# Attention and FFN on one core: the next pair's score products move behind the first FFN piece of the step

## The chip, the core and the metric

The kernel runs on one core of a Trainium2 chip. It uses the five engines of the core (TensorE for matrix products, VectorE, ScalarE, GpSimd, and SyncE, which here only issues transfers) and the 16 DMA engines. The metric is the device time of one execution in microseconds, lower being better. The kernel before takes 714.4 us, the median of three runs.

## The reference

Attention over 4 batches, 8 heads, 576 positions and 64 channels, with a bias that a small network of the distance of two positions makes for every head, and behind it a feed-forward network (FFN) on the 2304 tokens of 512 channels, with a hidden size of 2048:

```python
scores = scale * np.matmul(q, k.transpose(0, 1, 3, 2))
x = (np.log1p(np.abs(rel)) / psi_i)[..., None]
bias = np.maximum(x @ w1 + b1, 0.0) @ w2
scores = scores + bias.transpose(2, 0, 1)[None, :, :, :]
scores = scores - np.max(scores, axis=-1, keepdims=True)
attn = np.exp(scores)
attn = attn / (np.sum(attn, axis=-1, keepdims=True) + 1e-09)
x = np.matmul(attn, v)            # heads side by side: 2304 x 512
h = x @ w_in
g = h * np.clip(h + 3.0, 0.0, 6.0) / 6.0
out = g @ w_out
```

## The kernel before

**Tiles.** The 8 heads of a batch are taken two at a time (`PAIRS`). A unit is one batch, one pair of heads and either the first 256 query positions (4 tiles of 128 rows) or the last 320 (5 tiles). The 16 units of four tiles come first, then the 16 of five, 144 tiles in all. Tiles 2k and 2k+1 of a unit are the two heads of the same 128 positions, and their score products are made together, as a **pair** of tiles; the fifth tile of a long unit holds the last 64 positions of both heads and is a **single**. The order in a long unit is thus first pair, second pair, single.

**A step.** The main loop runs once for each tile number n. `front(n)` takes the row maximum of tile n on VectorE (`soft_max`, L561, which reads the scores out of PSUM together with the bias), emits the score products of the next pair if tile n+1 begins one (`qk_step(n + 1)`, L549 for tiles in two parts of fp32r, L527 for the first units), then normalizes tile n-1, makes the low half of tile n-2, sends tile n-3 through a transposing transfer (`soft_turn`, L637, issued by SyncE), and, where tile n-5 was the last of its unit, multiplies the unit's probabilities with v (`pv_step`, L704, **PV** below). `x_high` and `x_low` (L718 on ScalarE, L138 on VectorE) read PV's result a step later as two fp16 halves of x. Behind `front` the loop emits a part of the bias network where there is some left (`bias_step`, L864), and then pieces of the FFN: `rf` or `rf1` of them in a step (2.0, or 1.55 in the long units, carried over as `credit`). A piece is 12 matmuls: for the first half, one block of h (`h_ps`, L779), for the second, four blocks of the sum over the hidden size of an output block (`o_ps`, L802). `back(n)` does `x_high` and the exponential of tile n (L572).

**What sets the order.** Up to step 45 (`SWITCH`) a planner with a timeline of its own orders all engines. From then on, the steady part, TensorE runs in the order in which the program emits the work (`keep_order("PE")`), and from step 45 (`spn`) SyncE's queue does too. VectorE, ScalarE and GpSimd are still ordered by the planner. Each engine runs its list from top to bottom, and an instruction that waits holds up what is behind it.

**Banks.** In the steady part PSUM is split by `open_psum(ctx, 2, 4)`: two score tiles of two banks each, and four banks that h_ps, o_ps, PV and the bias take in turn. A pair takes both score tiles, a single one; they go round in turn. `reuse_waits="tile"` lets a tile be written again when all that read it is done: for a score tile that is L561, for PV's bank `x_low`, for h_ps L762 on VectorE.

Of the kernel before, what the change touches and what calls it, by code (L numbers as in the profile page):

```python
# [33 lines left out]
def attention_moe_kernel(  # L34
# [45 lines left out]
    def s_bank(name):  # L80
        return pools["ps_s"].tile([128, 2, 512], F32, tag="s", name=name)

    out_open = [False, 0]
    steady = [False]
    queue = []
# [423 lines left out]
    def at(n):  # L509
        return 0 <= n < NT  # L510
# [7 lines left out]
    def qk_step(n):  # L518
        b, p, t = tiles[n]
        i, s = ORDER[t]  # L520
        u = int(t >= 4)
        if direct(b, p, t):
            ps = s_bank("s_ps")
            q, k = qk_t[b, p, 0]
            c = 256 * s + 128 * i
            for a in range(2):
                nc.tensor.matmul(  # L527
                    out=ps[:, a, 0:HALF], lhsT=q[:, c:c + 128], rhs=k[:, a * HALF:(a + 1) * HALF]
                )
            s_t[n] = ps  # L530
            return
        if s:
            return
        if i == 4:
            hi, lo, tz = qk_t.pop((b, p, u))
            every = slice(0, 128)
            parts = [(every, tz[:, 0], tz[:, 1])]
        else:
            hi, lo = qk_t[b, p, u][:2]
            c = QC0[u] + 128 * i - 256 * u  # L540
            qs = slice(c, c + 128)
            parts = [(r, hi[r, qs], lo[r, qs]) for r in (slice(0, 64), slice(64, 128))]
        for k in range(len(parts)):
            s_t[n + k] = s_bank("s_ps")
        for k, (q, m) in enumerate(((0, hi), (0, lo), (1, hi))):
            for a in range(2):
                cs = slice(KC0[u] + a * HALF, KC0[u] + (a + 1) * HALF)
                for j, (rows, *w) in enumerate(parts):
                    nc.tensor.matmul(  # L549
                        out=s_t[n + j][:, a, 0:HALF], lhsT=w[q], rhs=m[rows, cs],  # L550
                        start=(k == 0), stop=(k == 2),
                    )

    def soft_max(n):
        b, p, t = tiles[n]
        i, s = ORDER[t]
        out, src = bt_t[b, p, i]
        bt, src = out[:, s * S:(s + 1) * S], src[s]
        ps = s_t.pop(n)[:, :, 0:HALF]
        sm = sm_p.tile([128, 4], F32, tag="sm", name="sm")  # L560
        nc.vector.tensor_tensor_reduce(  # L561
            out=halves(bt), in0=ps, in1=halves(src), op0=ALU.add, op1=ALU.min,
            scale=-0.125, scalar=3.0e38, accum_out=sm[:, 0:1],
        )
        a_t[n] = (bt, sm)
# [34 lines left out]
    def direct(b, p, t):  # L600
        return b < cfg["fb"] and t < 4
# [329 lines left out]
    def front(n):  # L931
        late = at(n + 1) and not direct(*tiles[n + 1])
        if at(n + 1) and not late:
            qk_step(n + 1)
        if at(n):
            soft_max(n)
        if n == START:
            open_ffn()
        if n == SWITCH:
            open_steady()  # L940
        if late:
            qk_step(n + 1)
        if unit_at(n - 6):
            x_low(*unit_at(n - 6))
        if at(n - 1):
            soft_norm(n - 1)
        if at(n - 2):
            soft_low(n - 2)
            if tiles[n - 2][2] in (1, 3, 5, 7, 8):
                freed[0] += 1  # L950
        if at(n):
            aux(n)
        if at(n - 3):
            soft_turn(n - 3)
        if unit_at(n - 5):
            pv_step(*unit_at(n - 5))
        while len(bt_t) - freed[0] < 4 and len(bt_t) < len(keys):
            k, b, p, i = keys[len(bt_t)]
            if k - n > cfg["la"]:
                break  # L960
            bias_until(256 if i < 2 else S)
            bt_t[b, p, i] = load_bias(b, p, i)
        if unit_at(n - 6) and unit_at(n - 6)[1] == PAIRS - 1:
            return unit_at(n - 6)[::2]
        return None

    def back(n):
        if unit_at(n - 5):
            x_high(*unit_at(n - 5))
        if at(n):  # L970
            soft_exp(n)
# [125 lines left out]
    def open_ffn():  # L1097
        nonlocal phase
        drain(gen_w)
        hidden_scale(0)  # L1100
        for c in range(KC):
            xv = x_t[0, 0][:, :, c]
            nc.vector.tensor_scalar(
                out=xv, in0=xv, scalar1=pscale["r1"][:, c:c + 1], scalar2=None, op0=ALU.mult
            )
        if cfg["fb"] > 1:
            x1 = const.tile([128, KC], F32, name="x1")
            nc.vector.tensor_scalar(
                out=x1, in0=pscale["r1"], scalar1=pscale["v1"][1], scalar2=None, op0=ALU.mult
            )  # L1110
            pscale["x1"] = x1
        stack_a.close()
        del pools["a"], pools["w"]
        pools["g"] = ctx.enter_context(tc.tile_pool(name="g", bufs=1, reuse_waits="tile"))
        pools["f"] = ctx.enter_context(tc.tile_pool(name="f", bufs=2, reuse_waits="tile"))
        queue.append(ffn(0, 0))
        phase = 1

    def open_steady():
        nonlocal phase  # L1120
        while phase < 2:
            ffn_step()
        stack_p.close()
        open_psum(ctx, 2, 4)
        steady[0] = True
        keep_order("PE")
# [27 lines left out]
    for n in range(-1, NT + 7):  # L1154
        if n < 7:
            next(gen_v, None)
        if n == cfg["spn"]:
            keep_order("SP")
        done = front(n)
        if phase == 0:  # L1160
            steps(gen_w, aw, cfg["rw1"])
        else:
            ao[0] += cfg["ro"]
            while ao[0] >= 1.0:
                ao[0] -= 1.0
                out_ready = not out_step()
        if phase and out_steps[0] >= cfg["bo"]:
            steps(gen_b, ab, cfg["rb"])
        if done is not None and done != (0, 0):
            b, u = done  # L1170
            queue.append(ffn(b, u))
        if queue:
            if phase == 1.5 and not out_ready:
                credit = cfg["gap"]
            else:
                credit += cfg["rf0"] if phase == 1 else cfg["rfo"] if phase < 2 else cfg["rf1" if unit_no[min(n, NT - 1)] >= 16 else "rf"]
            while credit >= 1.0 and queue and (phase < 2 or steady[0]):
                if ffn_step():
                    credit -= 1.0
                if phase == 1.5 and not out_ready:  # L1180
                    break
        back(n)
    for q_ in queue:
        drain(q_)
# [57 lines left out]
```

## Time and profile before

| | |
|---|---|
| median of three runs | 714.4 us (710.62 to 718.45) |
| the profiled execution's own time | 713.93 us |
| its span, first to last instruction | 712.1 us |
| TensorE matmuls busy | 657.8 us, 92% |
| VectorE, ScalarE, GpSimd busy | 498.2, 491.8, 257.0 us |
| h_ps matmuls (L779), o_ps matmuls (L802) | 198.6 and 196.6 us |
| mean granted TensorE clock | 0.976 |

The busy share is a mean over stages. The first 240 us make the bias, convert the weights and start the attention; the steady part follows up to about 600 us; then the rest of the FFN runs alone. In the rows below a time is counted from the start of the span, and an engine's idle time stands in brackets with what ended it.

### The profile page before, as it was taken

The numbers are of one execution on the slowest core, as the hardware profiler recorded it, in microseconds if no ns is written. First come the engines' busy times: TensorE is split into PE (matmuls) and PEld (weight loads), VectorE is DVE, ScalarE is ACT, GpSimd is POOL, SyncE is SP. The second block draws the span as 40 slices with busy tenths as digits, with TensorE's granted clock in tenths as the row PEclk, the third lists the DMA queues.
The fourth block names the chain that finished last, engine by engine and source line by source line (L and its number), as shares of the span: only waits on it lengthen the run. The fifth ranks groups of instructions, "written<-read, shape, count | busy, mean of one in ns | idle before, by whom it ended". The sixth has DMA issues, their size and how long they took to land. (4 is left out here: it accounts for less than half of the span.)

```text
span 712.1 us, 15431 instructions
## 1 busy us (share of the span) xinstructions
PE 657.8 (92%) x5538; PEld 471.2 (66%) x5538; DVE 498.2 (70%) x1263; ACT 491.8 (69%) x994; POOL 257.0 (36%) x350
## 2 busy tenths in 40 slices
PE   6667799898889998999998899999999999999998
PEld 2214566676466676788786788767776777777775
DVE  7999788899777697758866877777767776310310
ACT  6996678788676798758866876888568854631530
POOL 3212021346222154236642563465335611420420
PEclk9889999999999999999999999999999999999999
DMA  8987987856695996999999998969995865000000
GB/s 279 337 284 215 312 241 207 252 151 182 173 216 145 240 224 172 226 245 204 224 222 236 193 205 179 218 158 185 187 199 135 171 144 111 2 10 28 2 11 28
DMA packets 178637, 127.35 MB, mean 179 GB/s; under 512 B 139136, under 2 KB 147584, under 8 KB 178560
## 3 DMA queue, kind: packets, MB, share of 16 engines
q1 hardware_dynamic: 168768, 111.03, 67.0%
q10 hardware_dynamic: 9792, 15.34, 6.9%
q8 instruction: 43, 0.70, 0.4%
q14 instruction: 34, 0.28, 0.1%
HBM read 74.43 MB, written 15.34 MB: 126 GB/s over the span
## 5 line engine op out<-in xcount | busy, mean ns | idle before, releaser
L779 PE MATMUL h_ps<-x,wi 128*128 128x256 f16 (+1 forms) x1536 | 198.6, 287 | 8.0 <-DVE t L762 4.5
L802 PE MATMUL o_ps<-g,wo 128*128 128x256 f16 (+1 forms) x1536 | 196.6, 287 | 0.0
L779 PEld LDWEIGHTS <-wi 128*128 128x128 f16 x1536 | 147.1, 98 | 54.1 <-issue 12.3
L802 PEld LDWEIGHTS <-wo 128*128 128x128 f16 x1536 | 147.1, 98 | 47.0 <-issue 9.9
L758 POOL TENSOR_TENSOR g<-t,g 128x256 f16<-128x256 f32 (+1 forms) x128 | 101.9, 806 | 135.3 <-ACT g L756 134.4
L572 ACT ACTIVATE bt<-bt,sm 128x576 f32<-128x576 f32 x144 | 110.6, 768 | 56.1 <-DVE sm L561 55.3
L138 DVE SCALAR_TENSOR_TENSOR hl<-bt,sm,hl 128x576 f16<-128x576 f32 x112 | 98.7, 891 | 23.8 <-POOL hl L115 13.7
L762 DVE SCALAR_TENSOR_TENSOR t<-t,t,h_ps 128x320 f32<-128x320 f32 (+1 forms) x112 | 56.1, 516 | 68.4 <-ACT t L769 67.5
L115 POOL TENSOR_SCALAR hl<-bt,sm 128x576 f16<-128x576 f32 x56 | 48.9, 873 | 109.4 <-DVE sm L584 55.1
L864 PE MATMUL b_ps<-z,w_sb 128*32 128x288 f32 x576 | 68.5, 445 | 18.6 <-ACT z L851 15.5
L756 ACT ACTIVATE g<-t 128x256 f16<-128x256 f32 (+1 forms) x128 | 55.5, 440 | 35.3 <-DVE t L762 34.5
L404 POOL TENSOR_TENSOR qkl<-st,qkh 128x576 fp32r<-128x576 f32 (+2 forms) x48 | 56.1, 1188 | 43.9 <-ACT qkh L397 42.2
L769 ACT ACTIVATE t<-h_ps,t,hr 128x320 f32<-128x320 f32 (+1 forms) x112 | 64.7, 586 | 9.5 <-PE h_ps L779 6.3
L561 DVE CUSTOM_DVE_ANT_0 bt<-s_ps,bt 128x576 f32<-128x576 f32 x80 | 58.9, 751 | 10.3 <-PE s_ps L549 8.3
L864 PEld LDWEIGHTS b_ps<-z,w_sb 128*32 128x32 f32 x576 | 21.2, 113 | 54.1 <-ACT z L851 30.0
L812 ACT ACTIVATE ot<-o_ps,os 128x256 f32<-128x256 f32 (+1 forms) x32 | 15.9, 497 | 55.7 <-PE o_ps L802 54.7
L847 DVE TENSOR_SCALAR z<-T,nbp 128x576 f32<-128x576 f32 x85 | 51.0, 641 | 3.3 <-PE b_ps L864 3.2
L851 ACT ACTIVATE z<-T,bp 128x576 f32<-128x576 f32 x59 | 45.1, 767 | 11.7 <-PE b_ps L864 8.1
L561 DVE CUSTOM_DVE_ANT_0 bt<-s_ps,k 128x576 f32<-128x576 f32 x64 | 46.2, 752 | 6.3 <-PE s_ps L549 5.0
L527 PE MATMUL s_ps<-qk 128*128 128x288 f32 x128 | 41.2, 448 | 9.9 <-DVE sm L561 4.4
L121 ACT ACTIVATE hl<-bt,sm 128x576 f16<-128x576 f32 x56 | 43.1, 769 | 6.8 <-issue 1.5
L580 DVE TENSOR_SCALAR sm<-sm 128x1 f32<-128x1 f32 x112 | 16.8, 150 | 41.7 <-ACT bt L572 41.4
(118 smaller groups left out, 880.7 us busy)
## 6 DMA issues: line engine op xcount, KB each, us to landing
bt<-bias SPq DMA_DIRECT2D x64, 288.0 KB, 5.5
bias<-bo ACTq DMA_DIRECT2D x36, 288.0 KB, 4.8
w<-in_w_in_dram SPq DMA_DIRECT2D x16, 512.0 KB, 5.5
vs<-in_vp_dram SPq DMA_DIRECT2D x24, 320.0 KB, 5.1
st<-in_qk_dram SPq DMA_DIRECT2D x16, 448.0 KB, 4.4
wo<-in_w_out_dram SPq DMA_DIRECT2D x10, 512.0 KB, 7.1
k<-bias SPq DMA_DIRECT2D x32, 144.0 KB, 3.7
bt<-bias SPq DMA_DIRECT2D x32, 144.0 KB, 3.2
```

What stands on the lines that cost most here:

```text
L138: nc.vector.scalar_tensor_tensor(out=out, in0=full, scalar=scale, in1=high, op0=ALU.mult, op1=ALU.subtract)
L404: nc.gpsimd.tensor_sub(out=lo[:, c:c + w], in0=t[:, c:c + w], in1=hi[:, c:c + w].bitcast(F32))
L561: nc.vector.tensor_tensor_reduce(out=halves(bt), in0=ps, in1=halves(src), op0=ALU.add, op1=ALU.min, scale=-0.125, scalar=3.0e38, accum_out ...
L572: nc.scalar.activation(out=bt, in_=bt, func=AF.Exp, scale=-1.0, bias=sm[:, 0:1], accum_out=total)
L756: nc.scalar.activation(out=g[:, 0], in_=uu, func=AF.Copy)
L758: e.tensor_sub(out=g[:, 1], in0=uu, in1=g[:, 0])
L762: nc.vector.scalar_tensor_tensor(out=t_t[f], in0=t_t[f], scalar=cols(f)[2], in1=h_t.pop(f)[:, 0:n], op0=ALU.min, op1=ALU.mult,)
L769: nc.scalar.activation(out=t_t[f], in_=h_t[f][:, 0:n], func=AF.Relu, scale=cols(f)[0], bias=cols(f)[1],)
L779: nc.tensor.matmul(out=h_t[f][:, 0:n], lhsT=wi[:, a, c, f * 128:(f + 1) * 128], rhs=x[:, e, c], start=(k == 0), stop=(k == 3 * KC - 1),)
L802: nc.tensor.matmul(out=ops[:, 0:n], lhsT=wo[:, a, f, e * 128:(e + 1) * 128], rhs=g_t[f][:, r], start=(f == 0 and a == 0 and r == 0), stop= ...
L847: nc.vector.tensor_scalar(out=z, in0=src, scalar1=nbp[:, col], scalar2=None, op0=ALU.max)
L864: nc.tensor.matmul(out=pss[a][32 * k:32 * k + 32, 0:HALF], lhsT=w2_sb, rhs=z[:, a * HALF:(a + 1) * HALF],)
```

## The change

The call of `qk_step(n + 1)` leaves `front(n)` where the steady part has begun and there is FFN work in the queue. It is then made in the main loop behind the first FFN piece of the step, or behind the loop over pieces if that emits none. Where PV or bias matmuls belong to the step, they now come ahead of the scores as well.

```diff
@@ front(n) @@
         if n == SWITCH:
             open_steady()
-        if late:
-            qk_step(n + 1)
+        scores_due[0] = late
+        if late and not (steady[0] and queue):
+            scores_late(n + 1)
         if unit_at(n - 6):
             x_low(*unit_at(n - 6))
...
+    scores_due = [False]
+
+    def scores_late(n):
+        if scores_due[0]:
+            scores_due[0] = False
+            qk_step(n)
...
@@ the main loop, over the pieces of a step @@
                     credit -= 1.0
                 if phase == 1.5 and not out_ready:
                     break
+                scores_late(n + 1)
+        scores_late(n + 1)
         back(n)
```

On TensorE, in a long unit: the single of one unit (the rows with `tq`), the first pair of the next (`s_ps<-qkh` and the two rows behind it) and the PV (`pv_ps`) between them and the FFN (`h_ps`), before:

```order
L549 MATMUL s_ps<-qkh,tq_110 128x288 x2
L549 MATMUL s_ps<-qkl,tq_110 128x288 x2
...
L779 LDWEIGHTS wi
L779 MATMUL h_ps<-x,wi 128x256
...
L549 MATMUL s_ps<-qkh 128x288 x4
L549 MATMUL s_ps<-qkl,qkh 128x288 x4
L549 MATMUL s_ps<-qkh,qkl 128x288 x4
L704 LDWEIGHTS vh
L704 MATMUL pv_ps<-at,vh 64x320
```

and with the change:

```order
L549 MATMUL s_ps<-qkh,tq_110 128x288 x2
L549 MATMUL s_ps<-qkl,tq_110 128x288 x2
...
L704 LDWEIGHTS vh
L704 MATMUL pv_ps<-at,vh 64x320
...
L779 LDWEIGHTS wi
L779 MATMUL h_ps<-x,wi 128x256
L549 MATMUL s_ps<-qkh 128x288 x4
L549 MATMUL s_ps<-qkl,qkh 128x288 x4
L549 MATMUL s_ps<-qkh,qkl 128x288 x4
```

Before, one FFN piece and then the pair follow the single, and PV comes last; now PV stands right behind the single, one piece follows, and then the pair. The rest of the pieces come behind PV in the one case and behind the pair in the other.

On VectorE, at the same place of a later unit, whose FFN is in its first half (L561 is the maximum, the rows `x<-pv_ps` are `x_low`, `t<-t` is L762, which frees an h_ps bank), before:

```order
L561 ISA bt,sm<-s_ps,k_4261 128x576
L561 ISA sm 128x1
L138 SCALAR_TENSOR_TENSOR hl<-bt,sm,hl 128x576
...
L138 SCALAR_TENSOR_TENSOR vl<-vs,s_v_1494,vh 128x640
...
L138 SCALAR_TENSOR_TENSOR x<-pv_ps,xr,x 64x320
L138 SCALAR_TENSOR_TENSOR x<-pv_ps,xr,x 64x64
L138 SCALAR_TENSOR_TENSOR x<-pv_ps,xr,x 64x256
L762 SCALAR_TENSOR_TENSOR t<-t,t_2319,h_ps 128x320
```

and with the change:

```order
L138 SCALAR_TENSOR_TENSOR vl<-vs,s_v_1494,vh 128x640
L138 SCALAR_TENSOR_TENSOR x<-pv_ps,xr,x 64x320
L138 SCALAR_TENSOR_TENSOR x<-pv_ps,xr,x 64x64
L138 SCALAR_TENSOR_TENSOR x<-pv_ps,xr,x 64x256
L138 SCALAR_TENSOR_TENSOR hl<-bt,sm,hl 128x576
L561 ISA bt,sm<-s_ps,k_4247 128x576
L561 ISA sm 128x1
...
L762 SCALAR_TENSOR_TENSOR t<-t,t_2319,h_ps 128x320
```

The maxima of the first pair stood ahead of the three x rows, and now stand behind them.

## Rows read from the trace of the kernel before

**Rows 1.** Busy time by stretches: engines, granted clock, share of the 16 DMA engines.

```profile
core 0: us, PE busy (x) PEld busy (x) DVE busy (x) ACT busy (x) POOL busy (x), PEclk, DMA share, GB/s
240.00:300.00 60.00, 57.73 (x609) 40.94 (x607) 49.07 (x107) 52.72 (x109) 25.63 (x31) 1.00 0.90 211
300.00:360.00 60.00, 58.73 (x594) 49.59 (x591) 45.18 (x111) 44.28 (x99) 32.07 (x44) 1.00 1.08 225
360.00:460.00 100.00, 94.72 (x904) 78.23 (x902) 74.82 (x193) 72.11 (x160) 44.75 (x63) 0.98 1.01 209
460.00:600.00 140.00, 137.20 (x1158) 99.49 (x1157) 102.31 (x254) 99.95 (x213) 62.25 (x82) 1.00 0.79 163
...
380.00:400.00 20.00, 15.58 (x137) 12.76 (x135) 14.45 (x36) 13.40 (x31) 7.20 (x11) 0.91 1.12 241
```

**Rows 2.** Waits of TensorE and of its weight loads, 240 to 712 us.

```profile
PEld s_ps L549 <- DVE sm L561: 7.5, 7, 3.2
...
PE h_ps L779 <- DVE x L138: 3.3, 3, 1.6
PE h_ps L779 <- DVE t L762: 1.8, 1, 1.8
```

**Rows 3.** TensorE in order of time: start, length, matmuls, idle time before them.

```profile
338.80 0.40 PE L549 MATMUL s_ps<-qkh 64*128 64x288 f32 x1
...
341.37 1.17 PE L704 MATMUL pv_ps<-at,vh 128*64 128x256 f16 x18
...
384.01 0.43 PE L549 MATMUL s_ps<-qkh,tq 128*128 128x288 f32 x2
...
385.69 0.40 PE L549 MATMUL s_ps<-qkh 64*128 64x288 f32 x1
...
390.86 2.08 PE L704 MATMUL pv_ps<-at,vh 128*64 128x320 f16 x18
...
440.55 0.55 PE L549 MATMUL s_ps<-qkh,qkl 64*128 64x288 f32 x4
...
546.50 0.40 PE L549 MATMUL s_ps<-qkh 64*128 64x288 f32 x1
...
548.74 1.41 PE L704 MATMUL pv_ps<-at,vh 128*64 128x320 f16 x18
```

**Rows 4.** The chain that ended last, in order of time: an undisturbed stretch.

```profile
564.25 1.63 PE o_ps L802 x12
565.88 0.99 PE s_ps L549 x12
566.87 2.02 PE pv_ps L704 x28
```

**Rows 5.** TensorE in order of time: a piece with FFN, one with PV behind it.

```profile
562.45 1.80 PE L779 MATMUL h_ps<-x,wi 128*128 128x320 f16 x12
564.09 1.79 PE L802 MATMUL o_ps<-g,wo 128*128 128x320 f16 x12
...
598.57 1.80 PE L802 MATMUL o_ps<-g,wo 128*128 128x320 f16 x12
600.30 1.41 PE L704 MATMUL pv_ps<-at,vh 128*64 128x320 f16 x18
```

**Rows 6.** VectorE in order of time: a single's maximum, a pair's second one.

```profile
388.31 0.75 DVE L561 CUSTOM_DVE_ANT_0 bt<-s_ps,bt 128x576 f32<-128x576 f32 x1
...
443.67 0.75 DVE L561 CUSTOM_DVE_ANT_0 bt<-s_ps,k 128x576 f32<-128x576 f32 x1
```

**Rows 7.** TensorE in order of time: the longest wait for x.

```profile
465.25 1.80 PE L779 MATMUL h_ps<-x,wi 128*128 128x320 f16 x12 [1.64 <-DVE x L138]
```

**Rows 8.** Groups of matmuls by line and shape: busy us, mean ns, idle before.

```profile
L802 PE MATMUL o_ps<-g,wo 128*128 128x320 f16 x768 | 106.9, 300 | 0.0
```

**Rows 9.** SyncE's queue in order of time; landing of all transposes from 320 us on.

```profile
381.76 1.73 SPq L637 DMA_TRANSPOSE at<-hl  x1
...
DMA to landing us min/median/max: 2.8/4.3/7.0
```

## Prediction

> **What bounds the kernel now.** I read the page first, where TensorE is the busiest engine, then the busy time by stretches, then TensorE's waits, then TensorE in order of time. The table by stretches says how much is left to win where the change acts: from 240 to 600 us TensorE is busy 57.73 + 58.73 + 94.72 + 137.20 = 348.4 of 360 us, so 11.6 us are idle [rows 1]. From 600 us on no scores are left, and the first 240 us are in the older order of work; the change reaches neither. TensorE's waits in the steady part have three names: scores for the maximum on VectorE (7.5 us in 7 weight loads), h_ps for x on VectorE (3.3 us in 3 matmuls), h_ps for t (1.8 us in one) [rows 2]. In the order of time all seven score waits stand at one place of the five-tile unit: at its first pair, whose scores come one or two FFN pieces behind the last unit's single tile. The pair needs two score banks, and one of them is the single's, which is free only after VectorE has read it.
>
> **The waits that it takes away.** Undisturbed, a pair takes 0.99 us, the PV behind it 2.02, an FFN piece of 12 matmuls 1.63 (320 columns) [rows 4]. Seven first pairs take longer until their PV: the first is 338.80 to 341.37, the longest 385.69 to 390.86, the last 546.50 to 548.74 [rows 3]. Their excesses are 1.6, 4.2 and 1.25 us; the other four (0.5, 0.85, 0.55, 0.7, read in the same way) bring the sum to 9.6 us, a little above the 7.5 us that the weight loads waited, because the group also restarts. In the longest, TensorE stood for 3 us [rows 2], and the granted clock of that stretch is 0.91 in the mean, so part of it ran at the lower level, 1.2 GHz [rows 1]: the 18 PV matmuls at 390.86 take 2.08 us where those at 600.30 take 1.41 [rows 3, 5]. With that 0.6 the place is worth 10.2 us.
>
> After the change PV and one FFN piece come between the single and that pair, in place of one or two pieces the same number and the PV: 2.0 us more. The shortest distance is now 1.25 us (384.44 to 385.69 [rows 3]) and becomes about 3.4 us. How late is VectorE? In the worst case the single's maximum starts at 388.31 and ends at 389.06, 4.6 us behind its scores (384.01 + 0.43) [rows 3, 6]; all others are within the new distance. So only the worst keeps a wait, 4.6 - 3.4 = 1.2 us. **Gain 9.0 us.**
>
> The cover has a price: the pair is later, and from it to the unit's second pair only three pieces remain, without the PV: 3 x 1.63 = 4.9 us at 320 columns [rows 4], some 0.8 of it, 3.9, at 256. Both maxima of the pair must be over by then. The latest of these today ends at 443.67 + 0.75 = 444.42, 3.3 us behind its scores (440.55 + 0.55) [rows 3, 6]. That fits by half a microsecond, so I set nothing for it; it is the thinnest cover of the forecast.
>
> **x.** The three waits of h_ps for x are no wait for data: the fourth FFN piece behind a PV takes the PV's PSUM bank, which is free when VectorE has read it for the low part of x (1.64 us at 465.25 is the longest) [rows 7]. With the pair between PV and that piece there is 0.99 us more: 1.64 becomes 0.65, the others' 1.4 and 0.3 become 0.4 and nothing. **Gain 2.3 us.** VectorE's planned order also puts the x rows ahead of the pair's maxima where they came behind; that speaks for more, and I count nothing for it.
>
> **What it adds.** No instruction is added on any engine, and the loads and transposes on SP's queue stand in the same order. But TensorE changes its kind of work more often: pair and PV were neighbours 15 times, pair and bias matmuls 6 times, and now each has FFN ahead of it; 7 times PV comes straight behind the single. Counted in the order there are 14 more stretches of one kind from the steady part's start. A change costs little: 12 FFN matmuls with FFN behind them take 1.64 us (562.45 to 564.09), with a PV behind them 1.73 us (598.57 to 600.30) [rows 5]. So 14 x 0.1, and 0.05 for each PV behind a single: **cost 1.8 us.** The bounds are 0 (every change hidden) and a whole matmul of 0.30 us each time [rows 8], 4.2 us.
>
> The Trainium skill, "TensorEngine Tiling (Array Packing)", Key Properties, speaks against the change: switching the tiling mode drains TensorE, and the score pairs, the PV and the FFN use different modes. The 0.09 us above is what such a switch costs here; were each drain a whole matmul, the sum would come out at 710.3 instead of 707.9.
>
> **What may be late next.** PV comes one pair earlier and the single one piece later, so the last transpose of a unit has about 0.99 + 1.6 us less time before the PV that reads it. Where it was late, the wait removed covered it. A transpose lands 2.8 to 7.0 us behind the start of its issue, 4.3 in the median, that is some 2.9 us behind the issue's end [rows 9]. In all but three units the issue ended 4.6 us or more before PV's new place. The nearest: issued by 381.76 + 1.73 = 383.49, with PV's new place right behind the single, 384.44 [rows 9, 3]; the two others have 3.0 and 3.9 us in the same way. If the issue stays where it is, only the first waits, 2.0 us; if it moves with the single, the three wait 3.3, 1.2 and 0.6, together 5.1 us. I take the middle, **cost 3.5 us.**
>
> The other engines get a new order too, which their planner sets anew around the moved scores. A row of before cannot price that: the lower bound is the 11.6 us of idle time, beyond which nothing can be won, the upper the waits of the rivals. I leave it at 0 and in the range.
>
> **The sum**, against the profiled execution's own 713.9 us (span 712.1 and 1.8 around it): 713.9 - 9.0 - 2.3 + 1.8 + 3.5 = 707.9 us. The median of the runs, 714.4, is 0.5 above that execution, and the runs spread from 710.6 to 718.5; I forecast **708 us**.
>
> **Rivals.**
>
> *More comes free.* Transposes land in time, no score wait is left, and the x waits go too: 713.9 - 10.2 - 3.3 + 1.4 = 701.8, and 700 with the 1.8 us for t. For it: SP issues the transposes in an unchanged order, and from 460 us the DMA engines are busy only 0.79 [rows 1]. Against it: they are at 1.08 and 1.01 in the two stretches before, where the worst waits lie.
>
> *The work behind the waits was late, not the scores.* In the FFN's first half VectorE and ScalarE both carry its evictions. If the score wait only showed their lag, the lag shows again as a wait for an h_ps bank. Half of the 9.0 us and none of the 2.3 would be won: 713.9 - 4.5 + 1.8 + 3.5 = 714.7 us, no change. For it: ScalarE is busy 52.7 of 60 us from 240 to 300, and the waits for x and t are of this kind [rows 1, 2]. Against it: over the later stretches both engines are busy 71 to 75% [rows 1].
>
> *PV becomes the waiting one* (slower). From the point where a unit's last transpose lands behind the end of the next unit's single, TensorE, which keeps its order, stands at PV with FFN work behind it. At the median landing that is three places, as counted. Were each landing 7.0 us behind its issue's start, the waits would be 1.0, 3.9, 6.0 and 3.3 us in the four nearest units and none in the others, 14 us in place of 3.5: 707.9 + 10.6 = 718.5 us. With a lower granted clock behind the longest of them, or a second such stretch, it passes 721. For it: the DMA share of 1.0, and the cover that the score wait gave. Against: 4.3 us is the median, 7.0 a single extreme [rows 9].
>
> **How the numbers follow.** Forecast 0.50, for 703 to 712 us (switch costs 0 to 4.2, PV 2.0 to 5.1, and the planner's new order). More comes free 0.16, at 698 to 704. Lag shows elsewhere 0.20, at 711 to 717. PV waits 0.14, at 716 to 724. The range 701 to 717 leaves out some 0.05 below and 0.12 above. What a measurement here can tell from no change is about 1%, 7 us: faster means below 707.3, which takes all of the second case and half of the first, 0.41; slower means above 721.5, 0.08 from the last; within 1% the rest, 0.51.
>
> **What would show it.** Right: the weight loads' waits for scores behind the maximum shrink from 7.5 us to about 1; a first pair takes 1.0 us everywhere; PV appears as a waiter for transposes a few times between 360 and 460 us, 2 to 5 us in all; idle TensorE from 240 to 600 falls from 11.6 to some 4 to 6 us. Wrong: a wait at the unit's *second* pair (the half microsecond of cover was too thin), PV waits beyond 460 us, or new waits of h_ps for t.

## The result: 719.3 us against 714.2 us, and where the profile after puts it

The changed kernel takes 719.3 us in the median of 21 runs (714.1 to 726.4), the kernel before, on the same chip, 714.2 us (710.3 to 720.8). The ratio is 1.0068, with a 95% interval of 1.0049 to 1.0087. The change makes the kernel slower by 5 us. That is under the 1% that I called no change, but it is on the other side of the forecast of 708 us, and outside the range that ended at 717. The medians in this document take in every execution; a ratio leaves out those that took over 1.5% longer than the fastest of their kernel, for instance one of the 21 here and four of the twelve of e8 below.

One thing is needed to read the profiles. Single executions of either kernel lie 10 to 12 us apart, and the profiled execution of the changed kernel is its fastest (714.1 us, span 712.3). Its twin, the same file run again (721.1 us, span 719.3), is shown beside it as the second profile. Both order TensorE's work alike; they differ in the first 240 us, which the change does not touch (the steady part starts at 240.3 us in the one, at 244.0 in the other, at 243.6 before), and in one wait.

The waits first. This is the view of [rows 2] for the changed kernel, first profile (us in total, times, longest):

```profile
PE h_ps L779 <- ACT bo L880: 1.6, 2, 1.0
PE pv_ps L704 <- DMA at<-hl: 1.5, 1, 1.5
PE h_ps L779 <- DVE x L138: 0.8, 1, 0.8
PE h_ps L779 <- DVE t L762: 0.7, 2, 0.6
...
PEld s_ps L549 <- DVE sm L561: 12.2, 20, 1.5
```

and for its second profile:

```profile
PE pv_ps L704 <- DMA at<-hl: 4.4, 1, 4.4
...
PEld s_ps L549 <- DVE sm L561: 12.2, 20, 1.4
```

The waits for x went as forecast, from 3.3 us to 0.8 or none. Those for t fell too, from 1.8 us to 0.7, and waits of 1.6 us for ScalarE's output of the bias network (`bo`) are new. The weight loads' wait for scores did not shrink from 7.5 us to 1: it grew to 12.2 us, in 20 places in place of 7. And one PV waits for its transposes, 1.5 us in the one profile and 4.4 in the other. The stretches of [rows 1], in the second profile:

```profile
core 0: us, PE busy (x) PEld busy (x) DVE busy (x) ACT busy (x) POOL busy (x), PEclk, DMA share, GB/s
240.00:300.00 60.00, 57.77 (x613) 40.54 (x612) 46.10 (x107) 52.24 (x109) 24.44 (x31) 1.00 0.97 210
...
360.00:460.00 100.00, 90.41 (x842) 73.47 (x840) 76.44 (x182) 65.55 (x149) 41.48 (x57) 0.98 0.93 197
460.00:600.00 140.00, 137.47 (x1157) 98.45 (x1156) 104.39 (x256) 100.52 (x220) 67.40 (x88) 1.00 0.78 167
380.00:400.00 20.00, 14.31 (x125) 11.06 (x124) 13.02 (x35) 12.25 (x28) 7.23 (x11) 0.91 1.16 228
```

The loss is between 360 and 460 us: TensorE is busy 90.4 us there, before it was 94.7. In the other stretches it is busy within 0.8 us of before.

A second yardstick is free of the first 240 us: the length of the steady part, from the first row whose order the change touches to the start of the last PV but one, read from TensorE in order of time. It takes in the same matmuls in both. It is 356.7 us before (243.57 to 600.30), 360.2 in the first profile after (240.28 to 600.48) and 363.5 in the second (243.95 to 607.44): 3.5 and 6.8 us lost, with the medians' 5.0 between them.

Where do the new score waits stand? Here is TensorE in the second profile in order of time: the single and PV at the long stop, then a unit's two pairs.

```profile
387.34 0.43 PE L549 MATMUL s_ps<-qkh,tq 128*128 128x288 f32 x2
392.13 2.23 PE L704 MATMUL pv_ps<-at,vh 128*64 128x320 f16 x18 [4.37 <-DMA at<-hl]
...
429.72 0.53 PE L549 MATMUL s_ps<-qkh 64*128 64x288 f32 x4
...
430.71 4.11 PE L802 MATMUL o_ps<-g,wo 128*128 128x256 f16 x36
435.98 0.39 PE L549 MATMUL s_ps<-qkh 64*128 64x288 f32 x1 [1.17 <-DVE sm L561]
436.66 0.53 PE L549 MATMUL s_ps<-qkh 64*128 64x288 f32 x3 [0.28 <-DVE sm L561]
```

The pair at 429.72 is the unit's first, and it starts without a wait. Three pieces (36 matmuls) follow, and the *second* pair at 435.98 stands 1.17 us and then 0.28, because the first pair's maxima are not over. Read over the sixteen units, the time that a first pair's own run of scores lasts beyond 0.98 us falls from 9.7 us to 1.9 in all, at second pairs it rises from 0.2 to 4.9, and another 4.0 us of idle TensorE stand in front of second pairs, where before there was none.

VectorE in the same microseconds says why:

```profile
428.38 1.91 DVE L138 SCALAR_TENSOR_TENSOR hl<-bt,sm,hl 128x576 f16<-128x576 f32 x1
...
430.50 1.20 DVE L138 SCALAR_TENSOR_TENSOR vl<-vs,s_v,vh 128x640 f16<-128x640 f32 x1
433.14 0.82 DVE L138 SCALAR_TENSOR_TENSOR hl<-bt,sm,hl 128x576 f16<-128x576 f32 x1 [1.45 <-POOL hl L115]
433.88 1.25 DVE L138 SCALAR_TENSOR_TENSOR x<-pv_ps,xr,x 64x320 f16<-64x320 f32 x3
435.16 0.76 DVE L561 CUSTOM_DVE_ANT_0 bt<-s_ps,bt 128x576 f32<-128x576 f32 x1
435.84 0.75 DVE L561 CUSTOM_DVE_ANT_0 bt<-s_ps,bt 128x576 f32<-128x576 f32 x1
```

(hl and vl are the low halves of the probabilities and of v.) The scores are there at 430.7. VectorE takes vl first, stands 1.45 us for GpSimd's hl, takes hl and three x rows, and comes to the maxima at 435.16: the second ends 5.8 us behind its scores, and the three pieces cover them only until 430.71 + 4.11 = 434.8, some 4.0 us behind the scores. The same unit in the kernel before:

```profile
426.42 0.76 DVE L561 CUSTOM_DVE_ANT_0 bt<-s_ps,bt 128x576 f32<-128x576 f32 x1 [0.34 <-PE pv_ps L704]
...
427.10 0.75 DVE L561 CUSTOM_DVE_ANT_0 bt<-s_ps,bt 128x576 f32<-128x576 f32 x1
...
429.72 0.89 DVE L138 SCALAR_TENSOR_TENSOR vl<-vs,s_v,vh 128x640 f16<-128x640 f32 x1
...
431.99 1.25 DVE L138 SCALAR_TENSOR_TENSOR x<-pv_ps,xr,x 64x320 f16<-64x320 f32 x3
```

There the maxima come first and vl, hl and x behind them, under cover of PV and three pieces. The planner, which sees the scores one piece and a PV later, has put vl, hl and x ahead. Between the start of a first pair's scores and its first maximum, x rows run in fifteen of the sixteen units of the second profile, vl in 13 and hl in 12; before, hl runs there in 5, vl and x in none. Over the sixteen units the last maximum of a first pair ends 2.1 us behind its scores in the mean before (3.3 at most), 4.5 in the second profile (6.5 at most).

The groups of VectorE's rows from 320 to 600 us, kernel before (form and count, then busy us, mean ns, idle time before them and who ended it):

```profile
L138 DVE SCALAR_TENSOR_TENSOR hl<-bt,sm,hl 128x576 f16<-128x576 f32 x81 | 71.5, 893 | 19.5 <-POOL hl L115 11.3 <-ACT hl L121 7.4 <-DMA at<-hl 0.2
L561 DVE CUSTOM_DVE_ANT_0 bt<-s_ps,k 128x576 f32<-128x576 f32 x48 | 34.5, 752 | 3.4 <-PE s_ps L549 3.1
...
L138 DVE SCALAR_TENSOR_TENSOR vl<-vs,s_v,vh 128x640 f16<-128x640 f32 x16 | 15.4, 962 | 1.0 <-ACT vh L121 0.7 <-PE h_ps L779 0.3
```

and in the second profile after:

```profile
L138 DVE SCALAR_TENSOR_TENSOR hl<-bt,sm,hl 128x576 f16<-128x576 f32 x77 | 75.1, 997 | 19.7 <-ACT hl L121 11.3 <-POOL hl L115 8.1
L561 DVE CUSTOM_DVE_ANT_0 bt<-s_ps,k 128x576 f32<-128x576 f32 x46 | 32.9, 750 | 0.2
...
L138 DVE SCALAR_TENSOR_TENSOR vl<-vs,s_v,vh 128x640 f16<-128x640 f32 x16 | 15.9, 992 | 9.2 <-ACT vh L121 9.2
```

Before, VectorE waits for scores (3.1 us ahead of these maxima). After, that wait is gone, and 9.2 us of idle time sit in front of vl, for ScalarE's vh. Not all of that holds up a maximum. Read unit by unit in the order of time, VectorE is idle for 10.2 us while a first pair's scores are done and its maxima stand further down the list: 5.9 us of that in front of hl, 2.4 in front of vl, 1.3 in front of x and 0.6 in front of t. Before, it was 3.1 us, 1.8 of them in front of hl.

### The profile page after: what moved, and what is told of

It reads as the page before. It is cut to its first block, busy times and chain, and to the rows that moved or that the text cites. A ratio compares the mean times of both kernels' runs of the same rounds, so it can differ in the third digit from the quotient of the medians.

```text
span 712.3 us, 15422 instructions
## 1 busy us (share of the span) xinstructions
PE 657.1 (92%) x5538; PEld 467.2 (66%) x5538; DVE 503.8 (71%) x1263; ACT 488.5 (69%) x994; POOL 259.6 (36%) x350
## 5 line engine op out<-in xcount | busy, mean ns | idle before, releaser
L758 POOL TENSOR_TENSOR g<-t,g 128x256 f16<-128x256 f32 (+1 forms) x128 | 104.4, 822 | 124.5 <-ACT g L756 123.6
L138 DVE SCALAR_TENSOR_TENSOR hl<-bt,sm,hl 128x576 f16<-128x576 f32 x112 | 105.3, 958 | 25.6 <-ACT hl L121 13.2
L762 DVE SCALAR_TENSOR_TENSOR t<-t,t,h_ps 128x320 f32<-128x320 f32 (+1 forms) x112 | 56.9, 514 | 64.9 <-ACT t L769 64.0
L115 POOL TENSOR_SCALAR hl<-bt,sm 128x576 f16<-128x576 f32 x56 | 44.4, 793 | 120.5 <-DVE sm L584 55.8
L864 PE MATMUL b_ps<-z,w_sb 128*32 128x288 f32 x576 | 66.9, 448 | 19.4 <-ACT z L851 15.5
L561 DVE CUSTOM_DVE_ANT_0 bt<-s_ps,bt 128x576 f32<-128x576 f32 x80 | 59.0, 751 | 7.3 <-PE s_ps L549 5.6
L847 DVE TENSOR_SCALAR z<-T,nbp 128x576 f32<-128x576 f32 x85 | 46.4, 583 | 6.9 <-PE b_ps L864 3.7
L561 DVE CUSTOM_DVE_ANT_0 bt<-s_ps,k 128x576 f32<-128x576 f32 x64 | 46.0, 751 | 4.2 <-PE s_ps L549 3.0
```

Source lines behind the costliest of these rows:

```text
L115: nc.gpsimd.tensor_scalar(out=out, in0=full, scalar1=scale, scalar2=1.0, op0=ALU.mult, op1=ALU.mult)
L138: nc.vector.scalar_tensor_tensor(out=out, in0=full, scalar=scale, in1=high, op0=ALU.mult, op1=ALU.subtract)
L561: nc.vector.tensor_tensor_reduce(out=halves(bt), in0=ps, in1=halves(src), op0=ALU.add, op1=ALU.min, scale=-0.125, scalar=3.0e38, accum_out ...
L758: e.tensor_sub(out=g[:, 1], in0=uu, in1=g[:, 0])
L762: nc.vector.scalar_tensor_tensor(out=t_t[f], in0=t_t[f], scalar=cols(f)[2], in1=h_t.pop(f)[:, 0:n], op0=ALU.min, op1=ALU.mult,)
L864: nc.tensor.matmul(out=pss[a][32 * k:32 * k + 32, 0:HALF], lhsT=w2_sb, rhs=z[:, a * HALF:(a + 1) * HALF],)
```

## The experiments

The table sums up one profile each; its waits are those of the view of [rows 2], in us: weight loads for scores with the number of places, FFN for x and t together, PV for transposes. The last column is the length of the steady part. Times are medians, with the ratio to the kernel before on the same chip. All of the steady parts hold the same number of matmuls of each kind.

| kernel | time, ratio [95%] | scores | x, t | PV | steady part |
|---|---|---|---|---|---|
| before | 714.2 | 7.5 (7) | 5.1 | 0 | 356.7 |
| changed, first profile | 719.3, 1.0068 [1.0049, 1.0087] | 12.2 (20) | 1.5 | 1.5 | 360.2 |
| changed, second profile | 721.1 (one run) | 12.2 (20) | 0.7 | 4.4 | 363.5 |
| e2 PV ahead, no piece | 723.9, 1.0112 [1.0077, 1.0148] | 15.0 (20) | 2.7 | 0 | 363.1 |
| e3 piece ahead, no PV | 715.1, 1.0004 [0.9974, 1.0034] | 8.1 (7) | 3.7 | 0.4 | 357.5 |
| e4 second pair later | 716.1, 1.0005 [0.9978, 1.0031] | 3.6 (8) | 3.9 | 2.2 | 354.6 |
| e5 maxima ahead of x | 721.2, 1.0087 [1.0056, 1.0117] | 1.4 (4) | 8.2 | 4.4 | 361.8 |
| e6 maxima ahead of all | 736.7, 1.0318 [1.0284, 1.0352] | 0 | 6.4 | 15.1 | 375.4 |
| e7 half of PV ahead | 713.2, 0.9982 [0.9962, 1.0002] | 5.6 (7) | 2.0 | 2.1 | 355.2 |
| e8 the same, maxima ahead of all | 724.6, 1.0095 [1.0064, 1.0127] | 0 | 3.2 | 4.3 | 360.9 |
| e9 maxima ahead of x, 3 of 4 | 717.3, 1.0025 [0.9997, 1.0052] | 2.4 (7) | 4.2 | 5.4 | 360.4 |
| e10 20 of 28 of PV ahead | 713.9, 0.9980 [0.9949, 1.0011] | 5.8 (11) | 2.4 | 2.1 | 355.5 |

**Which part of the change does it (e1 to e4).** The change puts two things between the single and the first pair: the PV and a piece. e1 is the changed kernel again. The letters of the theories are those of each text; C means one thing in these four and another in e9.

> The changed kernel once more, for a second profile, since its first one (714.1 us) was the fastest of its 21 runs. Theory A (first pair's maxima stand behind the x rows on VectorE, so the second pair waits): from 240 to 600 us TensorE is idle more than in its first profile's 12.9 us, the waits of the score weight loads for the maximum are over 12 us, at second pairs; time near 719 us. Rival B (the loss lies before 240 us, where runs differ by themselves): the steady part is as long as before, and the first score group of the steady part starts some 5 us later than 243.

It ran in 721.1 us with the same waits; the first profile's quick start was luck.

e2 leaves the pieces behind the scores and moves only PV (and the bias matmuls) ahead of them: `scores_late` is called right behind the bias step.

```diff
             steps(gen_b, ab, cfg["rb"])
+        scores_late(n + 1)
         if done is not None and done != (0, 0):
```

> PV and the bias matmuls ahead of the scores as in the change, but the scores ahead of the first FFN piece as before. Theory A (distance from the first to the second pair without the PV is too short): slower than before by as much as the change, 0.4 to 0.9%. Rival C (the piece ahead makes the soft chain late for the transposes and for VectorE's list): as before, within 0.3%. Rival D (more changes of work on TensorE): some 0.2% slower.

e3 does the other half: the scores stand behind the first piece, and the PV stays behind the scores, as before.

```diff
-        if unit_at(n - 5):
-            pv_step(*unit_at(n - 5))
+        pv_due[0] = unit_at(n - 5)
+        if not scores_due[0]:
+            pv_late()
...
             qk_step(n)
+        pv_late()
```

> The scores behind the first FFN piece as in the change, and PV behind the scores as before (PV moves with them). Theory A: the distances between the pairs are those of before, so the time is that of before within 0.3%, with the waits at the first pair back. Rival C: slower by 0.4 to 0.9%, as the change. Rival D: as before.

e4 is the changed kernel with the second pair put back behind all pieces of its step, which gives the first pair's maxima their cover back.

```diff
-                scores_late(n + 1)
+                if not (at(n + 1) and tiles[n + 1][2] == 6):
+                    scores_late(n + 1)
```

> The change, with the second pair of a long unit behind all pieces of its step, one more FFN piece between first and second pair in about half of the units and one less between second pair and single. Theory A: the waits at those second pairs go; 2 to 4 us faster than the change, 715 to 717 us, unless the single then waits. Rival C or D: no gain over the change, 719 us or more.

The piece alone costs nothing (715.1 us, e3). PV ahead of the scores alone costs as much as the whole change or more (723.9 us; the intervals of the two ratios, 1.0112 and 1.0068, overlap a little). Giving the second pair its distance back takes the loss away (716.1, e4), and with it the score waits:

```profile
PE h_ps L779 <- DVE t L762: 3.0, 5, 1.1
PE pv_ps L704 <- DMA at<-hl: 2.2, 1, 2.2
...
PEld s_ps L549 <- DVE sm L561: 3.6, 8, 0.9
```

So it is the distance from the first pair to the second, from which PV was taken. The switches of work are not the loss: counted on TensorE from the start of the steady part, e4 has all 14 that the change adds, e3 has seven, and e2, the slowest of the four, has none. But e4 also shows that score waits are not simply lost time. They are 4 us fewer than before, waits of 2.2 us for transposes and of 3.0 for t came up, and its steady part is 2.1 us shorter. The time as a whole is that of before: in this profile the steady part starts at 246.1 us in place of 243.6, and one profile does not tell whether that goes with the edit.

**Is it VectorE's list (e5, e6)?** e5 queues the x rows behind the first pair's maxima on VectorE (`behind_max` is `tc.issue_after` of the last maximum); TensorE's order stays, row by row.

```diff
...
+        if steady[0] and at(n) and n + 1 in s_t and n + 1 not in a_t:
+            soft_max(n + 1)
...
         if unit_at(n - 6):
-            x_low(*unit_at(n - 6))
+            with behind_max():
+                x_low(*unit_at(n - 6))
```

> The changed kernel, with VectorE's three x rows of a unit queued behind the first pair's two maxima (and the second maximum of a pair emitted with the first); TensorE's order of the steady part is the changed kernel's. Theory A (the maxima are late because rows that wait for ScalarE and GpSimd stand ahead of them in VectorE's planned list): the first pair's last maximum ends about 1.5 to 2 us earlier behind its scores than in the second profile of the changed kernel, the score waits at the second pair fall from 5.4 us to 2 to 3, and the time is 715 to 717 us. Rival P (pace: without PV between the first pair and the second the two stand too close, whatever VectorE's list says, because vl and hl wait for the same engines): the maxima move by under 0.7 us, the waits at the second pair stay at 4.5 us or more, and the time is 718.5 to 721 us.

e6 does the same with vl (`split_v_b`) and hl (`soft_low`).

> As the run before, and vl and hl are queued behind the maxima too, at every group of scores in the steady part. Theory A: no maximum waits for another engine's rows any more; the score waits fall to 3 us or less in all, part of it comes back as PV waiting for the transposes (hl is later by two maxima, 1.4 us), and the time is 712 to 716 us. Rival P: the waits at the second pair stay at 4.5 us or more, 718 to 721 us. A third outcome, maxima early but the chain behind hl late (PV waits above 5 us), would give 718 us or more with few score waits.

The order on VectorE does decide about the score waits: 12.2 us became 1.4 and then nothing. In e5 the last maximum of a first pair ends 3.2 us behind its scores in the mean, 1.3 earlier than in the second profile of the changed kernel. That part of theory A is shown. Its times are refuted, 721.2 and 736.7 us, and for e6 the third outcome came. The waits of e5:

```profile
PE h_ps L784 <- DVE x L138: 6.3, 4, 2.7
PE pv_ps L709 <- DMA at<-hl: 4.4, 1, 4.4
...
PEld s_ps L549 <- DVE sm L561: 1.4, 4, 0.7
```

and of e6:

```profile
PE pv_ps L709 <- DMA at<-hl: 15.1, 7, 4.5
PE h_ps L784 <- DVE x L138: 4.2, 2, 3.5
```

What stood behind is now waited for: x by an FFN piece, and hl by its transposes and so by PV. In the sixteen five-tile units what the maxima gain the others lose: from the first pair of the first to the last single they take 281.1 us in e5 and 284.1 in e6, 282.8 in the second profile of the changed kernel. Most of the further loss of e6 lies elsewhere. Its list is forced at every group of scores of the steady part, and the four-tile units ahead take 10.6 us more than in that profile, with one wait of 3.5 us for x and one of 2.0 for t.

**Who pays where (e9).** The theory behind e9 was that an FFN reads x at once only where the last of a batch's four head pairs is done. e9 is e5 with the x rows left in front there.

```diff
+            last = unit_at(n - 6)[1] == PAIRS - 1
+            with nullcontext() if last else behind_max():
-            with behind_max():
                 x_low(*unit_at(n - 6))
```

> The changed kernel with the x rows queued behind the first pair's maxima, as in e5_max_before_x, but only for a unit's first three head pairs; at the last pair, whose x the next FFN reads at once, they keep their place ahead of the maxima. Theory C (one piece of VectorE's time is wanted by two: the scores' next pair wants the maxima, the FFN that starts wants the x rows, and only at the last head pair do both want it together): score waits at or below 5 us (second profile of the changed kernel: 12.7), x waits of TensorE at 1 to 3 us in place of 6.3, the wait of PV for its transposes as in the changed kernel (1.5 to 4.4), and the time is 714 to 717 us. Rival P (VectorE as a whole is late, so whatever is put behind is waited for): score waits fall but another wait (x, t or transposes) takes their place and the time stays at 718.5 to 721.

```profile
PE pv_ps L709 <- DMA at<-hl: 5.4, 1, 5.4
PE h_ps L784 <- DVE x L138: 2.1, 2, 1.4
PE h_ps L784 <- DVE t L767: 2.1, 2, 1.9
...
PEld s_ps L549 <- DVE sm L561: 2.4, 7, 0.7
```

Score waits of 2.4 us, x waits of 2.1 and 717.3 us, 0.3 above what theory C gave. By the medians that is 2 us better than the changed kernel (the two intervals just meet), and still not better than before. The longest wait left is PV's, 5.4 us, at the place where the kernel before has its own long stop. The reason that theory C gives does not hold, though. The two waits of e5 that are gone (2.7 us at 491.20 and 1.2 at 563.6) do come behind the PV of a last head pair, but the FFN that runs there is that of an earlier batch, whose x was done some 70 us before. What waits is the fourth piece behind that PV, which takes the PV's bank, and that is free when `x_low` has read it. That is the wait that the prediction describes for the kernel before.

**Dealing PV out (e7, e8, e10).** The kernel before has a short distance ahead of the first pair and a long one behind it. e7 splits the PV: 14 matmuls (`k < 7` of its 14 steps) ahead of the pair, 14 behind.

```diff
+        split = late and steady[0] and unit_at(n - 5)
+        if split:
+            pv_step(*split, 1)
         if late:
             qk_step(n + 1)
...
-            pv_step(*unit_at(n - 5))
+            pv_step(*unit_at(n - 5), 2 if split else 0)
```

> The kernel before, with the first 14 of a unit's 28 PV matmuls ahead of the first pair's scores and the other 14 behind them; FFN pieces stay where they were. If what decides is the distance from one group of scores to the next against the lag of the maxima (half of PV is worth 1.0 us): the wait at the first pair, 10.2 us in 7 units, falls by about 1.0 us in each of the 7, to 3 to 4 us; nothing comes up at the second pair, which still has half of PV and three pieces in front; 14 more switches cost 1.4 us and PV waits for transposes by up to 2 us more; the time is 708 to 713 us. If VectorE's list decides (the x rows and vl come ahead of the maxima as soon as PV starts earlier): the lags at the first and second pair rise by 2 us and the time is 715 to 719 us.

> The run before, with x, vl and hl rows queued behind the maxima as in the second of these runs. If both distance and list matter this is the best of the four: score waits under 3 us in all, 707 to 712 us. If only the distance matters it equals the run before; if hl behind the maxima makes PV wait for its transposes, it is 2 us or more above the run before.

e10 puts 20 ahead (`k < 10`).

> The kernel before with 20 of a unit's 28 PV matmuls ahead of the first pair's scores, in place of the 14 of e7_pv_halves. Theory of distances (a group of scores needs about 3 to 4 us from the one before it, and PV's 2.0 us can be dealt out between two distances): the first pair's waits fall from 6.7 us to 3 to 4 us and the second pair, which keeps 0.6 us of PV and three pieces, shows under 1 us; the time is 711 to 714 us. If PV's start ahead of the scores is what makes VectorE late (as in e2_pv_first with all 28, 723.9 us): maxima later by 1 us or more than in e7_pv_halves, waits at the second pair, and 716 to 720 us.

e7 and e10 came out at 713.2 and 713.9 us, at the upper end of what the theory of distances gave: nothing at second pairs, but the first pairs kept 6.7 and 5.3 us of the 9.7, since the singles' maxima became later by 0.9 and 1.2 us in the mean. They are the best kernels here, 0.2% under the kernel before, both with an interval that holds 1, so no gain over it is shown; against the changed kernel's median they win 5 to 6 us. e8 is slower by 1%, and its one profile is its fastest execution. In that profile the score waits are gone and the sixteen five-tile units take 273.2 us, against 275.2 before and 273.6 in e7; what is lost is lost in the four-tile units ahead of them (87.7 us in place of 81.5), where bias matmuls wait 4.9 us for VectorE. So e8 does not show that distance and list together lose at the first pairs.

**Is it the transposes (e11, e12)?** In the profiles of both kernels the longest stop of TensorE in the steady part lies between 384 and 392 us, where the DMA engines are full (share 1.12 before [rows 1], 1.11 and 1.16 after). In the kernel before, ScalarE waits there for a transpose, VectorE for ScalarE, and the single's maximum behind it starts at 388.31 [rows 6]:

```profile
386.31 0.56 ACT L769 ACTIVATE t<-h_ps,t,hr 128x256 f32<-128x256 f32 x1 [2.52 <-DMA at<-hl]
386.91 0.48 DVE L762 SCALAR_TENSOR_TENSOR t<-t,t,h_ps 128x256 f32<-128x256 f32 x1 [2.06 <-ACT t L769]
```

e11 and e12 are the kernel before and the changed one with no bias load in the steady part: one bias tile is used for all later score tiles, so other sums are computed, and the queues are lighter.

```diff
         src = [out[:, s * S:(s + 1) * S] for s in range(2)]
+        if steady[0]:
+            return out, kept[0, 1]
         if (p, i) in KEEP:
-            if b:
-                return out, kept[p, i]
```

> The kernel before, with no bias loaded in the steady part: one bias tile that is already there is used for every later score tile, so the sums are other ones and the DMA queues carry about a quarter less between 300 and 400 us. It is the base for the next run. If the long stop of TensorE at 386 to 391 us (the first pair's wait there, with hl waiting for a buffer that a late transpose holds) comes from the full DMA queues, it is gone here, with the fall of the granted clock behind it, worth 4 to 6 us; the first pair's other waits (5 to 6 us in 6 units) stay. If it comes from the engines' own order it stays, and the time of the steady part moves by under 2 us.

> The changed kernel with the same left out. If the loss of the change is VectorE's lateness (score waits moved to the second pair and doubled, 14 more switches), this run stays 3 to 6 us behind the run before it, with PV's wait for its transposes gone and the score waits still at 10 us or more. If the loss is PV waiting for its transposes in the stretch where the DMA queues are full, the two runs come within 2 us of each other.

The edit also takes away the reuse of kept bias tiles by later batches, so 62 bias loads in place of 47 are issued ahead of the steady part, and the first part is another one. Both are slower as a whole: 727.6 us (ratio 1.0169 [1.0112, 1.0226]) and 736.5 (1.0300 [1.0245, 1.0356]). What counts is the one against the other. e11 from 380 to 400 us, and its score waits:

```profile
380.00:400.00 20.00, 18.83 (x189) 15.66 (x189) 14.25 (x37) 13.87 (x32) 7.45 (x10) 1.00 0.93 189
```

```profile
PE s_ps L549 <- DVE sm L561: 4.2, 6, 1.3
...
PEld s_ps L549 <- DVE sm L561: 5.8, 7, 1.5
```

and e12:

```profile
380.00:400.00 20.00, 19.63 (x191) 16.18 (x190) 14.07 (x32) 11.62 (x26) 7.66 (x12) 1.00 0.83 165
```

```profile
PE s_ps L549 <- DVE sm L561: 5.5, 11, 1.2
...
PEld s_ps L549 <- DVE sm L561: 10.2, 18, 1.5
```

With the DMA share at 0.93 and 0.83 the long stop is gone in both, the granted clock there is 1.00, and no PV waits for transposes. The rest is unmoved: 7 short score waits before, 18 after. Against the kernel before, e11 has each of the sixteen five-tile units at its old length within 0.1 us, but for the one of the long stop. That one is 2.0 us shorter, and not by the 4 to 6 us that I expected; a wait for x behind it grew from 1.4 to 2.6 us. So the loss does not need the transposes; the long stop goes with the load on the DMA queues and is there in both kernels under different names. In the kernel before it is the first pair at 385.69 [rows 3], in the changed one PV at 392.13. The difference of 9 us is more than the 3 to 6 expected. The steady part holds 8.5 of it (360.8 and 369.3 us), its sixteen five-tile units 6.5 (272.2 and 278.7 us from their first scores to the start of their last single), of which 1.7 are a fall of the clock that is told in the last section. What else differs in the first units, behind first parts that are not alike, I did not follow.

## Why the prediction was wrong, step by step

**The waits it takes away: 9.0 us forecast, none won.** The first pairs do start in time (9.7 us of excess to 1.9, forecast about 1). But the step behind it, the price of the cover, failed: "The cover has a price ... That fits by half a microsecond, so I set nothing for it". I compared the new cover of 3.9 to 4.9 us with the old lag of 3.3 us at most. The lag is itself a result of the order: with the scores later, vl, hl and x stand ahead of the maxima, and the lag became 4.5 us in the mean and 6.5 at most. In the sixteen five-tile units the groups of scores, with the idle time ahead of them, now take 12.3 us beyond their undisturbed lengths, where they took 9.9. The sign that I had named, a wait at the unit's second pair, is what the trace shows.

**x: 2.3 us forecast, 2.5 to 3.3 won.** Right in size. But I wrote that the x rows ahead of the maxima speak "for more". It was the same VectorE time, counted on the wrong side: e5 gives it to the maxima, and TensorE then waits 6.3 us for x, in 721.2 us.

**Switches: 1.8 us forecast.** The 14 came, seven of them in the sixteen five-tile units. Where the scores do not wait (e5) they cost about 1 us there, by the lengths of the FFN's stretches; an FFN piece with PV behind it is again some 0.1 us longer. The Trainium skill, "TensorEngine Tiling (Array Packing)", Key Properties, speaks of a drain at a switch of the tiling mode. The rows show no larger price than this, and do not tell whether it is that drain.

**PV behind its transposes: 3.5 us forecast (2.0 to 5.1), 1.5 and 4.4 measured.** Right in place, and in size in the second profile; the first is below the bounds. It is no loss of its own against the kernel before, since the same stop stood there at the first pair; I had booked its removal as 4.2 of the 9.0 us and its return as a cost. The two units around it take 36.1 us before, 33.7 and 37.7 in the two profiles after, so the change wins 2.5 us there or loses 1.6, and this one stop is the difference between the two profiles. In the other fourteen units the change loses 6 to 7 us in both.

**The other engines' new order: set at 0.** This is the term that decided, and it was put at nothing without a price. The planned list of VectorE could be read ahead of any run: in the changed kernel vl, hl and three x rows stand ahead of most first pairs' maxima, five rows, and 4.7 us of work and waits in the unit shown (430.50 to 435.16). I read it for x only and did not put the rows into the lag.

Set against undisturbed lengths (pair 0.98 us, single 0.88, PV 2.02 or 1.65 and twelve FFN matmuls 1.60 or 1.32, by columns), the sixteen five-tile units of the second profile lose, each kind with the idle time ahead of it: scores +2.5, PV +5.2, FFN -0.3 (h_ps -2.3, o_ps +2.0), together 7.4 us, where they last 7.6 longer (274.1 and 281.7 us from their first scores to the start of their last single). In the first profile it is +2.4, +0.9 and +0.7, together 4.0, where they last 4.3 longer. The four-tile units of the steady part are 0.8 us shorter in both. The score term stands at only 2.5 because the long stop has left it for PV: without that stop's 4.2 us it rises from 5.7 us to 12.3.

Of the rivals, "the work behind the waits was late, not the scores" came nearest: VectorE's lag does show again at another place. But it looked for it at the h_ps banks, where the waits became fewer, and not at the second pair, and its price of 714.7 us was too small.

## What to carry to other kernels

A wait for a PSUM bank is the difference of two numbers, a distance on TensorE and a lag on the engine that empties the bank. An edit that moves the work changes both, so the lag has to be worked out anew from the other engine's new list, row by row with its waits, before it is set against the new cover. And where waits wander from scores to x to transposes when one is removed, as in e4, e5 and e6, the engine that empties the banks has little slack at that place. Here giving the distance back (e4) or dealing it out (e7, e10) took the loss away, and another order of that engine won 2 of the 5 us at best (e9).

## What the hardware showed that I had not expected

VectorE's hl row of 128x576 takes 0.82 us at 433.14 above, beside no more than a memset on GpSimd, but 1.91 us at 428.38, while GpSimd runs its subtraction for qkl. From 300 to 600 us rows of hl above 1.0 us number 15 before and 29 in both profiles after, 6.4 and 14 us in all beyond 0.82 each, and the vl of the unit shown takes 1.20 in place of 0.89. Every one of the long rows runs beside a row of GpSimd, but so do about twenty of the 53 short ones in the second profile. The Trainium skill, "SBUF — State Buffer", section "SBUF: two separate sides", says that a VectorE instruction with two SBUF inputs and a GpSimd instruction that reads SBUF lock each other out of a shared port; these rows agree. It makes VectorE later, but does not decide by itself: e4 and e10 have 27 and 28 such rows and are level with the kernel before. How much of the new lag it is, no run here tells.

The granted clock fell once without a long stop. In e12 36 FFN matmuls at 456.46 us take 5.77 us where the 36 at 449.51 take 4.11, behind a wait of 1.2 us and two of 0.8 and 0.5 in the 25 us ahead of it, and the clock from 456 to 460 us is 0.63, so most of that time ran at the lower level, 1.2 GHz:

```profile
449.51 4.11 PE L802 MATMUL o_ps<-g,wo 128*128 128x256 f16 x36
454.79 0.40 PE L549 MATMUL s_ps<-qkh 64*128 64x288 f32 x1 [1.18 <-DVE sm L561]
...
456.46 5.77 PE L802 MATMUL o_ps<-g,wo 128*128 128x256 f16 x36
```

The same place of the changed kernel, with the same wait of 1.17 us (435.98 above), kept the full clock: its 36 matmuls at 437.65 take 4.10 us, and the clock from 436 to 440 us is 1.00. So that wait alone does not lower the clock, and what made the difference stays open.
